# Deferring the dV products of the last head group by two macro steps in an attention backward kernel

## The chip, the cores and the metric

The kernel runs on one core of one Trainium2 chip. The metric is the device time of the program in microseconds; lower is better.

The names are those of the profile: PE is the engine that multiplies matrices, DVE the vector engine, ACT the scalar engine; POOL issues the stores here. A matmul writes into a bank of the memory called PSUM, and an eviction is the copy by DVE or ACT that empties the bank. The granted clock is the share of the full PE clock that the trace records.

## The reference, cut to what matters

The program computes a forward and a backward pass through two rounds of grouped-query attention with a long key/value cache, each followed by an MLP, with shared weights.

```python
def _A_ref(x, k_cache, v_cache, wq, wo):          # B=2, Hq=32, Hkv=4, Sk=16384, Dh=128
    q = (x @ wq).reshape(B, Sq, Hq, Dh)...
    scores = einsum("bhqd,bhkd->bhqk", q, k) * (Dh ** -0.5)
    p = softmax(scores)
    o = einsum("bhqk,bhkd->bhqd", p, v)
    return o... @ wo

x = x + A(layernorm(x)); x = x + B(layernorm(x))  # and both once more
out, vjp = jax.vjp(f, A_x, A_k_cache, A_v_cache, A_wq, A_wo, B_w1, B_b1, B_w2, B_b2)
return (out, *vjp(grad_out))                      # dK and dV: 2 x 4 x 16384 x 128 bf16 each
```

The two cache gradients are 33.5 MB each (2 x 4 x 16384 x 128 x 2 bytes); all outputs together are the 98.6 MB that the profile counts as written.

## The kernel before

The last part of the kernel walks over 32 chunks: 8 pairs of batch and key/value head ("groups"), 4 chunks each, of 4096 key positions. Chunk 31 is the last chunk of the last group. For every chunk it must

- transpose V, form the scores of the gradient (`dp`) and from them `dX`,
- sum dq from `dX` and K (`dq_quad`), and once per group reduce it (`Acc.reduce`),
- form dK and dV of the chunk (`kv_pair`, in two halves) and store 1 MB each.

When both groups of a head are reduced, that head's quarter of dWq can be formed (16 products of 512 columns, `dw_units`) and the gradient that flows on to x (`dn`, 64 matmuls). After the loop comes the backward of the first layer norm and one last small output row.

A half of dK or dV is eight matmuls into four PSUM banks, then four evictions, shared by ACT and DVE. A dWq product is one matmul into one bank and one eviction. All of them take their banks in turn from the same four:

```python
X = [px([128, 512], F32, "xm%d" % i) for i in range(4)]
def mx():
    return nxt("x", X)                            # round robin

def kv_pair(w, i, h):                             # half h of dK or dV of chunk i
    ...
    pss = [mx() for _ in range(4)]
    for b in range(2):
        for r in range(4):
            PE.matmul(pss[r][:, b * 256:(b + 1) * 256], lhsT=blk[32 * r:32 * r + 32, o + 2 * h + b, :],
                      rhs=Qm[...], start=True, stop=True, tile_position=(32 * r, 0))        # L1159
    for r in range(4):
        evac_cast(sv_[:, 2 * h:2 * h + 2, r], pss[r][:]..., 512)                          # L156 ACT, L159 DVE
    if h == 1:
        store(...)                                                                        # L982, 1 MB
# dw_units: one product
    ps = mx()
    PE.matmul(ps[:], lhsT=xrows[p:p + 4, ...], rhs=yrows[p:p + 4, ... 512 columns])          # L1018
    evac_cast(sv_[:, j, c0:c0 + 512], ps[:], 512)
```

The main loop, one macro step per turn. `v_at` says at which step a dV chunk starts, `k_at` the same for dK:

```python
v_at = {2 * i - 3: i for i in range(2, NC)}       # NC = 32 chunks, NCH = 4 per group
k_at = {(i if i < NCH else 2 * i - NCH): i for i in range(NC)}
while 2 * m < NS + 12 or late or fill or late_pe or m <= max(v_at) + 2:
    ...
    for k in range(2):
        ...                                       # transposes of V, scores; dX of a chunk
        if late_pe and (k == 1 or s >= NS):
            late_pe.popleft()()                   # among others the 64 dn matmuls (L847)
        at, w, m_ = ((k_at, "K", m - 1), (v_at, "V", m))[k]
        for h in range(2):
            if at.get(m_ - h) is not None:
                kv_pair(w, at[m_ - h], h)
    ...
    make_blks(iv, ik)                             # transposes the coefficients of the next dV, dK (L1134)
    sch.run_slot(1)                               # the dq work due in this step; the reduce (L426)
    step_fill(1 if m < NCH else 5)                # up to five dW products
    m += 1
g0 = attn_in_bwd(0, g1, dn0)                      # layer norm backward, then the last output row (L195)
```

In the kernel before, the last dq is reduced at the end of step 59; the halves of dV chunks 28 to 31 run in steps 53 to 60.

Of the kernel before, what the change touches and what calls it, by code (L numbers as in the profile page):

```python
# [23 lines left out]
def kernel(  # L24
# [42 lines left out]
    NCH = T // TC  # L67
# [965 lines left out]
    NC = len(chunks)  # L1033
# [248 lines left out]



    v_at = {2 * i - 3: i for i in range(2, NC)}
    k_at = {(i if i < NCH else 2 * i - NCH): i for i in range(NC)}
    NS = (NC - NCH) * NB
    m = 0
    while 2 * m < NS + 12 or late or fill or late_pe or m <= max(v_at) + 2:
# [6 lines left out]
        for k in range(2):  # L1296
            s = 2 * m + k
            if s < NS:
                i, b = NCH + s // NB, s % NB
# [57 lines left out]
```

## Time and profile before

| | kernel before |
|---|---|
| time, median of the first 3 runs | 1173.21 us (1172.8 to 1175.07) |
| read, written | 348 MB, 98.6 MB; DMA 383 GB/s on average |
| last load landed | 1128.6 us |
| last but one reduce of dq, last reduce | 1112.48 us, 1146.22 us |
| issue of the last output row, end | 1168.05 us, 1172.1 us |

First, stretches of the trace of the kernel before. The columns are the stretch, its length, busy time (and count) of PE, PE weight loads, DVE, ACT and POOL, then the granted TensorE clock, the DMA share and GB/s.

```profile
1119.50:1122.70 3.20, 3.19 (x66) 2.24 (x64) 2.33 (x4) 2.09 (x5) 0.53 (x1) 1.00 1.00 412
1122.70:1127.10 4.40, 4.11 (x79) 2.95 (x81) 3.96 (x8) 3.71 (x8) 0.53 (x1) 1.00 1.03 430
...
1112.48:1146.22 33.74, 27.60 (x429) 17.20 (x429) 26.11 (x44) 24.33 (x48) 4.27 (x8) 0.84 1.01 423
...
1146.22:1156.38 10.16, 7.73 (x96) 4.61 (x97) 4.47 (x11) 3.90 (x8) 0.53 (x1) 0.50 0.48 198
1156.38:1161.90 5.52, 5.27 (x12) 1.52 (x11) 4.16 (x8) 4.07 (x8) 1.30 (x2) 0.50 0.92 374
```

Up to the last reduce (1146.22) the DMA is full. Behind it, it is not: between 1146 and 1156 its share is 0.48. The DMA view of the last 32 us, in 40 slices of 0.8 us, shows the hole:

```profile
GB/s 410 430 430 430 420 420 420 461 399 430 379 317 317 225 72 82 51 41 31 20 31 389 430 430 348 399 451 271 379 404 369 323 394 394 287 26 5 0 10 0
```

Seven slices, 5.6 us, are below 150 GB/s. The stores explain it. This is the timeline of POOL, which issues them (start, duration, what; in brackets how long POOL had been idle and what ended that):

```profile
1141.38 0.53 POOL L982 DMA_DIRECT2D out_dram<-keepxK  x1 [4.88 <-DVE keepxK L159]
1143.26 0.53 POOL L982 DMA_DIRECT2D out_dram<-keepK  x1 [1.35 <-ACT blk L148]
1155.81 0.53 POOL L982 DMA_DIRECT2D out_dram<-keepV  x1 [12.02 <-DVE keepV L159]
1157.69 0.53 POOL L982 DMA_DIRECT2D out_dram<-keepK  x1 [1.34 <-ACT big L156]
1159.53 0.77 POOL L982 DMA_DIRECT2D out_dram<-big  x1 [1.31 <-ACT big L156]
1162.58 0.77 POOL L982 DMA_DIRECT2D out_dram<-big  x1 [2.27 <-ACT big L156]
1168.05 0.55 POOL L195 DMA_DIRECT2D out_dram<-o_row  x1 [4.70 <-DVE o_row L194]
```

For 12 us POOL has nothing to store, because the engines are on the chain behind the last dq: reduce, rows of dq, dWq, dn. The chain of waits says the same (start, duration, what):

```profile
1146.22 1.03 PE xm L426 x4
...
1147.86 1.02 PE tpm L949 x8
1148.88 0.02 issue
1148.91 0.59 ACT rowsA L148
1149.49 0.04 issue
1149.54 1.86 PE xm L1018 x4
1151.40 1.82 PE xm L847 x64
1153.22 0.74 PE xm L1159 x7
...
1156.39 3.91 PE xm L1018 x9
```

The twelve last dWq products run back to back; the timeline of PE has them as one line, 12 in 5.27 us:

```profile
1156.39 5.27 PE L1018 MATMUL xm<-rowsA,rowsB 4*128 4x512 bf16 x12 [0.49 <-ACT keepK L156]
```

### The profile page before, as it was taken

To read this page: it belongs to the slowest core of one execution; us is meant where nothing else is said; L and a number is where in the kernel's file an instruction comes from. 1 tells how busy PE (TensorE), PEld (TensorE's weight loads), DVE (VectorE), ACT (ScalarE), POOL (GpSimd) and SP (SyncE) were. 2 spreads that over 40 slices of the span, in tenths; PEclk is the share of its full clock that TensorE was granted. 3 is DMA by queue.
4 is the path that set the end of the run, shared out by engine and by line. 5 is a ranking of instruction groups with operands and counts; after the bars stand their busy time and mean duration, and the time that the engine had idled before them with its cause. 6 is when DMAs were issued, how large, how long until landed. Compare 5 with 4: busy or idle time off the path is not lost. (4 is left out here: it accounts for less than half of the span.)

```text
span 1172.1 us, 40218 instructions
## 1 busy us (share of the span) xinstructions
PE 968.7 (83%) x17709; PEld 743.1 (63%) x17709; DVE 627.2 (54%) x1319; ACT 555.1 (47%) x1395; POOL 63.9 (5%) x113
## 2 busy tenths in 40 slices
PE   4988885497879876899987889888898999898886
PEld 3866673487767755888775688755555554555452
DVE  1544451133545433454845434567777877886774
ACT  0544441022535430344454434367667867786673
POOL 0000000000000000000000000001111111111111
PEclk9988885587989975999997899888777867887785
DMA  9999999998999989989999989677999999999996
GB/s 370 415 417 416 418 417 396 395 356 351 416 417 413 416 329 416 390 320 398 387 410 411 352 320 338 254 271 322 361 403 419 414 417 421 418 421 418 422 423 263
DMA packets 89131, 449.32 MB, mean 383 GB/s; under 512 B 7026, under 2 KB 7026, under 8 KB 49788
## 3 DMA queue, kind: packets, MB, share of 16 engines
q1 hardware_dynamic: 72204, 348.17, 74.5%
q0 software_dynamic: 16752, 98.59, 20.5%
q8 instruction: 138, 2.26, 0.8%
q14 instruction: 37, 0.30, 0.1%
HBM read 348.14 MB, written 98.58 MB: 381 GB/s over the span
## 5 line engine op out<-in xcount | busy, mean ns | idle before, releaser
L148 ACT COPY kT<-tp 128x512 int32<-128x512 int32 x204 | 120.0, 588 | 254.5 <-PE tp L379 246.6
L151 DVE COPY kT<-tp 128x1024 bf16<-128x1024 bf16 x164 | 112.1, 690 | 117.1 <-PE tp L379 106.9
L379 PE MATMUL tp<-ident,kv_K 128*128 128x128 bf16 x1728 | 144.2, 232 | 4.2 <-DMA kv_K<-in_A_k_cache_dram 4.1
L379 PEld LDWEIGHTS <-kv_K 128*128 128x128 bf16 x1728 | 109.6, 104 | 5.0 <-DMA kv_K<-in_A_k_cache_dram 4.7
L159 DVE CAST big<-xm 128x512 bf16<-128x512 f32 x141 | 91.9, 686 | 33.6 <-PE xm L1018 15.9
L156 ACT CAST big<-xm 128x512 bf16<-128x512 f32 x156 | 84.8, 595 | 24.2 <-PE xm L1018 14.7
L532 PEld LDWEIGHTS <-kT 128*128 128x128 bf16 x2048 | 76.6, 98 | 28.3 <-issue 22.3
L532 PE MATMUL sc<-qT_bf,kT 128*128 128x8 bf16 x2048 | 92.1, 171 | 0.7 <-issue 0.7
L263 PE MATMUL wtp<-ident,wt 128*128 128x128 bf16 x928 | 79.3, 235 | 3.8 <-issue 2.4
L379 PE MATMUL tp<-ident,kv_V 128*128 128x128 bf16 x864 | 72.9, 233 | 9.9 <-DMA kv_V<-in_A_v_cache_dram 8.3
L297 PEld LDWEIGHTS <-wt 128*128 128x128 bf16 x1696 | 48.9, 103 | 45.8 <-issue 14.7
L496 ACT ACTIVATE e_all<-sc,negm 128x64 bf16<-128x64 f32 x256 | 77.2, 345 | 1.1 <-DVE negm L491 1.0
L411 PE MATMUL acc_all<-kv_V,e_all 128*16 128x256 bf16 x864 | 46.4, 295 | 28.4 <-DMA kv_V<-in_A_v_cache_dram 15.4
L148 ACT COPY wT<-wtp 128x512 int32<-128x512 int32 (+1 forms) x60 | 34.5, 576 | 74.1 <-PE wtp L263 65.4
L151 DVE COPY wT<-wtp 128x1024 bf16<-128x1024 bf16 (+1 forms) x64 | 40.5, 637 | 52.7 <-PE wtp L263 49.3
L159 DVE CAST keepK<-xm 128x512 bf16<-128x512 f32 x92 | 59.9, 685 | 16.3 <-PE xm L1159 9.4
L156 ACT CAST keepK<-xm 128x512 bf16<-128x512 f32 x105 | 56.2, 593 | 23.3 <-PE xm L1159 21.1
L379 PEld LDWEIGHTS <-kv_V 128*128 128x128 bf16 x864 | 57.5, 104 | 11.8 <-DMA kv_V<-in_A_v_cache_dram 9.2
L263 PEld LDWEIGHTS <-wt 128*128 128x128 bf16 x928 | 60.7, 105 | 4.6 <-issue 3.1
L156 ACT CAST keepV<-xm 128x512 bf16<-128x512 f32 (+1 forms) x98 | 53.3, 595 | 20.3 <-PE xm L1159 17.0
L496 ACT ACTIVATION_READ_ACCUMULATOR e_all<-sc,negm 128x1 f32 x256 | 60.1, 235 | 0.0
L159 DVE CAST keepV<-xm 128x512 bf16<-128x512 f32 (+1 forms) x74 | 48.5, 686 | 20.3 <-PE xm L1159 16.1
(335 smaller groups left out, 1776.2 us busy)
## 6 DMA issues: line engine op xcount, KB each, us to landing
kv_K<-in_A_k_cache_dram SPq DMA_DIRECT2D x81, 1024.0 KB, 12.9
kv_V<-in_A_v_cache_dram SPq DMA_DIRECT2D x81, 1024.0 KB, 12.6
out_dram<-big POOLq DMA_DIRECT2D x36, 1024.0 KB, 17.7
wt<-in_A_wo_dram SPq DMA_DIRECT2D x32, 1024.0 KB, 11.0
wt<-in_B_w_dram SPq DMA_DIRECT2D x32, 896.0 KB, 14.4
out_dram<-keepK POOLq DMA_DIRECT2D x22, 1024.0 KB, 17.6
out_dram<-keepV POOLq DMA_DIRECT2D x18, 1024.0 KB, 17.7
wt<-in_A_wq_dram SPq DMA_DIRECT2D x16, 1024.0 KB, 9.3
```

The source lines that it names most:

```text
L148: S.copy(out=dst.bitcast(I32), in_=src.bitcast(I32))
L151: V.tensor_copy(out=dst, in_=src)
L156: S.copy(out=dst, in_=src)
L159: V.tensor_copy(out=dst, in_=src)
L263: PE.transpose(tp[:, o, :], wv[:, j, (o0 + o) * 128:(o0 + o + 1) * 128], ident[:])
L297: PE.matmul(fps[:, jo, :].rearrange("p (a b) -> p a b", b=2), lhsT=wv[:, j, jo * 128:(jo + 1) * 128], rhs=xT_bf[:, j0 + j, :].unsqueeze(1) ...
L379: PE.transpose(tp[:, j, :], cv[:, b * 8 + j, :], ident[:])
L411: PE.matmul(self.acc[cg:cg + 16, :], lhsT=coef(u), rhs=self.cv[:, t:t + 2, :].rearrange("p t d -> p (t d)"), start=False, stop=True, tile_ ...
L496: S.activation(out=e_all[:, g, f * half:(f + 1) * half, l, h, :], in_=sc[g][f][:, h, :].rearrange("p (a b) -> p a b", b=2), func=ACT.Exp, ...
L532: PE.matmul(sc[g][f][:, :, t % TH], lhsT=kT[:, j, :], rhs=q_bf[:, g, :], start=True, stop=True)
```

## The change

The intent: take the dV products of the last group out of the way of the last dq, so that the chain behind dq starts earlier, and let them run behind it.

```diff
-    v_at = {2 * i - 3: i for i in range(2, NC)}
+    v_at = {2 * i - 3 + (2 if i >= NC - NCH else 0): i for i in range(2, NC)}
```

The eight halves of chunks 28 to 31 move from steps 53 to 60 to steps 55 to 62. The last reduce stays in step 59. Seven of them were issued before it; now five are.

## The prediction

> **What bounds the kernel now.** Over the whole span the DMA engines are full (page, slices: DMA 9 tenths in nearly all). Only the end differs. In the table by stretches, 1000 to 1140 us has a DMA share of 1.01 to 1.03, 1140 to 1150 0.97, 1150 to 1160 0.45, 1160 to 1172 0.65. By the DMA records the last load has landed at about 1128.6 us, and from then to 1149 the stores drain a backlog at 1 MB per 2.47 us. The queue is empty from about 1149 to 1156: the timeline shows dK/dV stores issued at 1141.4 and 1143.3, the next one at 1155.8, then 1157.7, 1159.5 and 1162.6. The tail is a serial chain, not bandwidth: last dq (1146.2) -> dq rows (rowsA 1148.9) -> dWq products, 64 dn matmuls (1151.3 to 1153.2), the last dK and dV halves, the rest of dWq (12 matmuls, 1156.4 to 1161.7, one per 0.43 us), layer norm, output row issued at 1168.05. The last dWq store lands about 1168.2, the row 1169.3.
>
> **What the change does.** No arithmetic is added or removed. Of each of the four dV chunks of the last group, the two halves (8 matmuls, 4 evictions each) run two macro steps later. Net: two dV halves and four coefficient transposes leave the steps at about 1119 to 1127 us, and two halves go behind the last dq, between the dWq products; their coefficients get an eviction of their own.
>
> **Gain.** In 1119.5 to 1127.1 PE is busy 3.19 of 3.20 and 4.11 of 4.40 us, ACT and DVE about 80%. Two halves take 0.40 to 0.69 us of PE each, the four transposes 0.38, the eight evictions 2.1 us of ACT and 2.6 us of DVE in parallel. Estimate: the last dq is reached 2.3 us earlier (1.4 to 3). Loads cannot hold it up: the last K chunk has landed 9 us before its use at 1137.75.
>
> **Cost.** Behind dq the granted clock is 0.5 and the dWq products already hold PE at 5.26 of 5.6 us. A half put between them needs the four PSUM banks that dWq uses, 0.61 us of matmuls and 1.07 (ACT) or 1.29 us (DVE) of evictions. In 1136 to 1146 such a half takes about 1.75 us. Estimate: 1.6 us each, and 0.4 us for the separate coefficient transposes: 3.6 us.
>
> **Sum.** The tail ends about 1.3 us later. The DMA gap gets shorter (stores restart at about 1153.5 instead of 1155.8), but 5 MB instead of 4 MB then remain: at the 2.7 us per MB of the tail it ends near 1169, so bandwidth gives nothing.
>
> The clock: the records switch between 0.5 and 1.0 in multiples of 3.413 us, as the Trainium skill has it ("TensorE: Matmul & The Clock Gate", Part 1). The drop at 1138.8 may fall one window earlier or later against the work; I allow half a microsecond.
>
> **Prediction: 1174.5 us, 1171.5 to 1177.0 in 8 of 10. Faster by over 2%: 0.01; within 2%: 0.98; slower by over 2%: 0.01.**
>
> **Right if:** reduce of the last dq starts at about 1144; the dK store follows at 1153 to 1154; each dV half among the dWq products costs 1.4 to 1.8 us; the last dWq store is issued at 1163.5 to 1164.5; the DMA gap shrinks by 2 to 3 us, with the span no shorter.
>
> **Wrong if:** the removed halves free 3 us or more before dq (then about 0, or a small gain); the dV halves fill waits among the dWq products for nearly nothing (gain of up to 2 us); the clock stays at 1.0 in the tail.

## The result and the profile after

The changed kernel took 1177.39 us (median of 4, 1175.98 to 1178.91), the kernel before 1174.14 us in its 4 runs. The ratio is 1.0027 with a 95% interval of 1.0006 to 1.0049. A second measurement with more rounds gave 1.0045 (1.0022 to 1.0068). Ratios here are the mean time of one kernel's fast runs over that of the other's fast runs of the same rounds, so they are not quite the ratio of the medians quoted. So the change is slower, by some 3 to 5 us, well within 2%.

The same stretches, cut at the same events, of the changed kernel:

```profile
1114.74:1146.43 31.69, 26.61 (x410) 16.09 (x410) 23.45 (x40) 21.74 (x44) 3.72 (x7) 0.86 0.99 411
...
1146.43:1156.71 10.28, 8.10 (x100) 4.83 (x101) 4.74 (x12) 3.96 (x8) 0.53 (x1) 0.50 0.20 80
1156.71:1166.90 10.19, 8.03 (x28) 2.32 (x27) 7.37 (x13) 6.20 (x12) 1.83 (x3) 0.50 0.78 309
```

Its timeline of PE over the last dWq products:

```profile
1156.71 2.29 PE L1018 MATMUL xm<-rowsA,rowsB 4*128 4x512 bf16 x5
1158.39 1.22 PE L1159 MATMUL xm<-QmV,blkv 32*128 32x256 bf16 x3
1159.78 0.58 PE L1159 MATMUL xm<-QmV,blkv 32*128 32x256 bf16 x5 [0.17 <-DVE big L159]
1160.91 2.35 PE L1018 MATMUL xm<-rowsA,rowsB 4*128 4x512 bf16 x5 [0.55 <-ACT keepxV L156]
1162.65 1.22 PE L1159 MATMUL xm<-QmV,blkv 32*128 32x256 bf16 x3
1164.04 0.58 PE L1159 MATMUL xm<-QmV,blkv 32*128 32x256 bf16 x5 [0.17 <-DVE big L159]
1165.16 1.01 PE L1018 MATMUL xm<-rowsA,rowsB 4*128 4x512 bf16 x2 [0.55 <-ACT keepxV L156]
```

And its stores, and the DMA view from 1140 us to the end (40 slices of 0.93 us):

```profile
1156.02 0.53 POOL L982 DMA_DIRECT2D out_dram<-keepV  x1 [12.23 <-DVE keepV L159]
1157.80 0.53 POOL L982 DMA_DIRECT2D out_dram<-keepK  x1 [1.25 <-ACT blkv L148]
1159.49 0.76 POOL L982 DMA_DIRECT2D out_dram<-keepK  x1 [1.15 <-ACT keepK L156]
1166.34 0.53 POOL L982 DMA_DIRECT2D out_dram<-keepxV  x1 [6.09 <-DVE keepxV L159]
1167.45 0.76 POOL L982 DMA_DIRECT2D out_dram<-big  x1 [0.58 <-issue]
1172.98 0.53 POOL L195 DMA_DIRECT2D out_dram<-o_row  x1 [4.77 <-DVE o_row L194]
```

```profile
GB/s 381 292 328 416 425 407 416 416 142 106 44 27 27 44 18 27 27 0 275 416 407 319 425 407 328 376 390 58 0 151 416 425 323 390 381 182 5 0 9 0
```

What the reader is to see:

- From the last but one reduce to the last: 31.69 us instead of 33.74. The steps ahead of the last dq did get shorter.
- From the last reduce to the next dWq products, 10.28 instead of 10.16 us: nothing gained, nothing lost.
- Then the twelve products. In the kernel before they take 5.5 us with their evictions. Here two halves stand between them, and it takes 10.2 us. The start of the sixth product of the stretch is 2.54 us behind the fifth (11.94 and 14.48 us behind the reduce, in the trace's instruction records) where it is 0.43 us in the kernel before. So one half costs 2.11 us.
- The store of the last dWq part goes out 21.0 us behind the reduce (1167.45 less 1146.43) instead of 16.4.
- The hole in the DMA did not shrink. It grew: ten slices of 0.93 us below 150 GB/s, 9.3 us, and a second hole near 1166 us. Counted in the same way in three traces of each program (table below), the first hole is 5.6, 6.4 and 6.4 us before and 9.3, 7.4 and 9.3 us with the change.

Three traces of each program give the sizes. (The third trace with the changed order is the experiment without the last dV store, below, whose engines do the same.)

| us | before | change |
|---|---|---|
| start of the last but one reduce (nothing differs up to there) | 1112.48, 1117.85, 1114.42 | 1114.74, 1116.43, 1118.89 |
| from it to the last reduce | 33.74, 33.94, 33.94 | 31.69, 32.66, 32.73 |
| from the last reduce to the issue of the output row | 21.83, 21.85, 21.84 | 26.55, 26.56, 26.56 |
| sum of the two | mean 55.71 | mean 58.92 |
| from the issue of the row to the end | 4.10 in all three | 4.07, 4.07, 4.01 |

The first row is scatter that the change has no part in, 1112 to 1119 us. The third row repeats to 0.02 us. The difference of the sums, +3.2 us, is the effect by the traces: 1.5 us less ahead of the last dq, 4.7 us more behind it.

The 1.5 us need not all be due to the order. In the three traces of the kernel before, the granted clock is 0.5 for one stretch of 3.41 us just behind the last but one reduce, and in the third trace of the change too (32.73 us). In the first two traces of the change there is no such stretch (31.69 us, and 32.66 us with a wait for a load that is shown below). Compared under the same clock the gain is 33.87 less 32.73, 1.1 us; that is one trace of the change. The part behind the last reduce runs at 0.5 throughout in all six.

### The profile page after: what moved, and what is told of

Same layout as the page of the kernel before. It is cut to its first block, busy times and chain, and to the rows that moved or that the text cites. A ratio compares the mean times of both kernels' runs of the same rounds, so it can differ in the third digit from the quotient of the medians.

```text
span 1177.1 us, 40223 instructions
## 1 busy us (share of the span) xinstructions
PE 970.7 (82%) x17709; PEld 740.9 (63%) x17709; DVE 628.3 (53%) x1320; ACT 553.7 (47%) x1395; POOL 63.7 (5%) x113
## 5 line engine op out<-in xcount | busy, mean ns | idle before, releaser
L159 DVE CAST big<-xm 128x512 bf16<-128x512 f32 x137 | 89.3, 685 | 26.7 <-PE xm L1159 13.0
L156 ACT CAST big<-xm 128x512 bf16<-128x512 f32 x152 | 82.2, 593 | 23.0 <-PE xm L1018 11.1
L379 PE MATMUL tp<-ident,kv_V 128*128 128x128 bf16 x864 | 70.4, 228 | 8.0 <-DMA kv_V<-in_A_v_cache_dram 6.4
L263 PEld LDWEIGHTS <-wt 128*128 128x128 bf16 x928 | 59.7, 104 | 5.4 <-issue 4.0
```

Source lines behind the costliest of these rows:

```text
L156: S.copy(out=dst, in_=src)
L159: V.tensor_copy(out=dst, in_=src)
L263: PE.transpose(tp[:, o, :], wv[:, j, (o0 + o) * 128:(o0 + o + 1) * 128], ident[:])
L379: PE.transpose(tp[:, j, :], cv[:, b * 8 + j, :], ident[:])
```

## The experiments

Theory P (place): a dV half is cheap where it was and dear where it went, because among the dWq products it has to share four PSUM banks with them and each waits for the other's evictions. Rival W (write bandwidth): more stores are left when the queue restarts, and writing them ends the program. Rival D (drift): the profiled run of the change was 2.3 us late at the last but one reduce already, so there may be no effect at all.

### The change again

> The changed kernel again, to size the effect with more rounds. Theory P (place: two dV halves cost about 2.05 us each among the dWq products plus 0.6 us for their own coefficient transposes, 4.7 us in all, and give back only about 2.05 us before the last dq): +2.6 us, ratio 1.0022, and in the profile 31.7 us from the reduce of the last dq but one to that of the last (33.7 in the kernel before), then 26.5 us to the issue of the output row (21.8 before). Rival W (write bandwidth: 5 MB instead of 4 MB left when the stores restart): about the same total, but the last row would have to wait for stores, not for engines. Rival D (drift: the profiled run of the change was already 2.3 us late at the last dq but one, where nothing has changed yet): ratio within 1.000 to 1.001.

Measured: 1180.88 us (median of 6), the kernel before 1174.06 us, ratio 1.0045 (1.0022 to 1.0068). In the trace 32.66 us between the reduces and 26.56 us from the last one to the row. The tail is as expected to 0.1 us; the gain ahead of it is smaller. One line of the waits of PE in this stretch names an item that the first trace did not have:

```profile
PE tpm L1304 <- DMA keepK<-in_A_v_cache_dram: 1.2, 1, 1.2
```

PE had got ahead of a load of V and waited 1.2 us for it. D falls: the ratio is outside its 1.000 to 1.001.

### Only the last chunk later

```diff
-    v_at = {2 * i - 3: i for i in range(2, NC)}
+    v_at = {2 * i - 3 + (2 if i == NC - 1 else 0): i for i in range(2, NC)}
```

> The kernel before with the last dV chunk alone two macro steps later. P: nothing is taken out of the busy steps at 1119 to 1127 us; one half leaves the step of the last dq (worth about 1.7 us), one the step after it (about 1.7), two go among the dWq products (4.1 us) with 0.6 us of transposes: +1.3 us (0.7 to 2). W: 4 MB remain at the restart as in the kernel before, so 0 to +0.3 us.

Measured: ratio 0.999 (0.9964 to 1.0015), which decides nothing. The trace does more: 31.79 us between the reduces, 24.78 us to the row, 56.57 in sum, +0.9 us against the kernel before, inside P's range and above W's. The two halves stand in the dWq products exactly as in the change:

```profile
1159.13 2.29 PE L1018 MATMUL xm<-rowsA,rowsB 4*128 4x512 bf16 x5
1160.81 1.22 PE L1159 MATMUL xm<-QmV,blkv 32*128 32x256 bf16 x3
1162.20 0.58 PE L1159 MATMUL xm<-QmV,blkv 32*128 32x256 bf16 x5 [0.17 <-DVE big L159]
1163.32 2.35 PE L1018 MATMUL xm<-rowsA,rowsB 4*128 4x512 bf16 x5 [0.55 <-ACT keepxV L156]
```

Again 2.54 us from product to product (10.16 and 12.70 us behind the reduce). One half has left the step behind the reduce, so the first product of the stretch starts 8.50 us behind it instead of 10.16 in the kernel before. That is 1.66 us less; against the change, which also has the separate coefficient transposes there, it is 1.78 us less (10.28). So a half costs about 1.7 to 1.8 us there, with the next half waiting for it, and 2.1 us is more than that.

### Six PSUM banks in the tail, changed kernel

```diff
         sch.s = m
         qs = []
+        if m == 2 * NC - 5:
+            X.extend(t[:].bitcast(F32).rearrange("p a b -> p (a b)") for t in TP)
         iv, ik = v_at.get(m + 1), k_at.get(m)
```

`TP` are the two banks that the transposes use; hardly any are left in the tail.

> The changed kernel with six PSUM banks instead of four in rotation from the step of the last dq on. P with the PSUM round trip as its mechanism: a dV half among the dWq products no longer waits for their evictions and they not for its own; it costs 1.0 to 1.3 us instead of 2.05, so 1.5 to 2 us less than the change, about +0.5 to +1 us against the kernel before. If a half cost what its matmuls and evictions take, whatever the banks: no change, +2.6 us. W: no change, +2.6 us.

Measured: 1175.76 us against 1180.88 for the change on the same chip in the same rounds; ratio to the kernel before 1.0002 (0.9979 to 1.0024). From the last reduce to the row 23.74 us instead of 26.56. The timeline of PE over the first half among the dWq products:

```profile
1154.69 0.63 PE L1018 MATMUL xm<-rowsA,rowsB 4*128 4x512 bf16 x1
1154.71 0.90 PE L1159 MATMUL xm<-QmV,blkv 32*128 32x256 bf16 x2
1155.25 0.39 PE L1159 MATMUL tpm<-QmV,blkv 32*128 32x256 bf16 x2
1155.26 0.56 PE L1159 MATMUL xm<-QmV,blkv 32*128 32x256 bf16 x2
1155.62 1.06 PE L1018 MATMUL xm<-rowsA,rowsB 4*128 4x512 bf16 x2
```

From 1154.69 to 1155.62 it is 0.93 us from product to product, instead of 2.54; the half costs 0.5 us. The waits for the evictions in brackets, of 0.17 and 0.55 us, are gone. The work is the same: same matmuls, same evictions, same clock of 0.5. So 1.6 of the 2.1 us were waits for a PSUM bank, not work. The expectation for the half (1.0 to 1.3 us) was still too dear.

### Six banks, kernel before

The same edit in the kernel before.

> The control: six banks in the kernel before. The three halves and the dWq products behind the last dq go a little faster: 0.5 to 1 us less than the kernel before. P with round trips: the distance between the two placements falls from 2.6 to at most 1.7 us. W: 0, and the distance stays at 2.6.

Measured: ratio 0.9984 (0.9957 to 1.0011); 20.46 us from the last reduce to the row instead of 21.84. (Behind the last dq there are two halves ahead of the twelve products, not three.) The expected 2.6 and 1.7 us were differences of the whole. From the last but one reduce to the row the difference of the two placements is 54.56 - 53.23 = 1.3 us with six banks and 3.2 with four, as expected; but only the trace of `before_six` has the stretch of half clock ahead of the last dq, so part of this is not the banks. From the last reduce to the row alone it is 23.74 - 20.46 = 3.3 us with six banks and 4.7 with four. Of these 3.3 us the two halves are 1.0, the last product to the row 0.8 (7.83 against 7.02), and the rest is the first dWq product behind the coefficient transposes: it starts 10.19 us behind the reduce against 8.75 in the kernel before, 1.4 us more, where the difference was 0.1 us with four banks. The transposes now share their bank with the rotation, and in `after_six` this product waits for their eviction:

```profile
1153.03 0.58 PE L1018 MATMUL tpm<-rowsA,rowsB 4*128 4x512 bf16 x1 [0.69 <-ACT blkv L148]
```

What the six banks save in the tail is not all saved in the total. The row of `before_six` is issued at 1164.10 us and the program ends 6.18 us later instead of 4.10 (5.48 in `after_six`):

```profile
1164.10 0.55 POOL L195 DMA_DIRECT2D out_dram<-o_row  x1 [4.71 <-DVE o_row L194]
```

In its packet records the row's packets are done by 1165.7 us, and a single chain of 4 KB packets runs on alone to 1167.5. So with a tail only 1.4 us shorter the stores already end the program in this trace: from the last but one reduce to the end it takes 59.41 us, against 59.66 to 59.89 in the kernel before.

### Six banks after the coefficient transposes

The edit above with `m == 2 * NC - 3`, two steps later.

> The changed kernel with the two further PSUM banks in rotation only one macro step before the end, after the coefficient transposes that use one of them. If the costs add as read: a dV half among the dWq products delays them by 0.5 us instead of 2.1, and the transposes stay at 0.1 us, so 23.3 us (22.9 to 23.8) from the last reduce to the issue of the output row, against 26.56 in the change and 21.83 in the kernel before.

Measured: 24.68 us, 0.9 us above the top of the expected range. The transposes stay at 0.1 us as expected, and the second half costs 0.56 us. But the first half costs 1.36: when it comes, the four old banks have just been taken by dWq products and only the two new ones are free, so it waits for evictions again. The miss agrees with the mechanism: which banks are free when the half comes counts, not the number of banks alone.

### No store of the last dV chunk

The changed kernel without one store of 1 MB. Its result is wrong: the last chunk of dV stays unwritten.

```diff
             dst = dVv if w == "V" else dKv
+            if (w, i) == ("V", NC - 1):
+                return by_store.append(stgs[w, i])
             store(dst[g, :, c * TC:(c + 1) * TC, :], ...)
```

> The changed kernel without the store of the last dV chunk (1 MB; the result is wrong on purpose, the chunk stays unwritten). W: 2.5 us less than the change, back to the kernel before. P: the engines' chain is untouched, within 0.5 us of the change, so +2 to +2.6 us against the kernel before.

Measured: ratio 1.0042 (1.0014 to 1.0069), no faster than the change; 26.56 us from the last reduce (1151.62) to the row, then 4.0 us to the end. Its last stores:

```profile
1172.64 0.76 POOL L982 DMA_DIRECT2D out_dram<-big  x1 [7.20 <-issue]
1178.18 0.55 POOL L195 DMA_DIRECT2D out_dram<-o_row  x1 [4.77 <-DVE o_row L194]
```

The last dWq store goes out 21.02 us behind the reduce, as in the change, although one megabyte less is written. W falls as an explanation of the change.

### The dq work first in each of the last steps

```diff
+            if m > NS // 2 and k == 0:
+                sch.run_slot(1)
             at, w, m_ = ((k_at, "K", m - 1), (v_at, "V", m))[k]
 ...
-        sch.run_slot(1)
+        if m <= NS // 2:
+            sch.run_slot(1)
         step_fill(1 if m < NCH else 5)
```

> The kernel before, with the dq work of each of the last steps issued ahead of that step's dK and dV halves instead of behind them. P (the tail is a serial chain with idle gaps of 3.3 us between the last dq and the first dWq eviction): two halves fill that gap, 2 to 3 us less than the kernel before. W (the tail is bound by writing): at most 1 us less.

Measured: ratio 0.9987 (0.9962 to 1.0011). In the trace 30.04 + 23.87 = 53.91 us, 1.8 us less than the kernel before's 55.71. The direction is P's; the size is a little under its range.

### The last dq one step earlier

`dq_first`, and both quads of the last chunk in the same step:

```diff
-        sch.later(2, lambda: dq_quad(i, 1))
+        n = 1 if i == NC - 1 else 2
+        sch.later(n, lambda: dq_quad(i, 1))
         if c == NCH - 1:
-            sch.later(2, accs[g].evac)
-            sch.later(3, accs[g].reduce)
+            sch.later(n, accs[g].evac)
+            sch.later(n + 1, accs[g].reduce)
```

> As dq_first, and the last dq sums both its quads one macro step earlier, so that dWq runs among the last dK and dV halves. P: 3 to 5 us less than the kernel before; the idle gap of the stores shrinks, by the DMA records, from 6.6 to under 4 us. W: at most 1 us less.

Measured: 1173.60 us, ratio 0.9975 (0.9947 to 1.0002). From the last but one reduce to the end 57.8 us, against 59.7 to 59.9 in the three traces of the kernel before: 2.0 us less, not 3 to 5. The hole in the stores is still 5.7 us in this trace (slices below 150 GB/s). A dK half and a dV half now stand between the fifth and the sixth of the twelve products, which start 4.33 us apart: about 1.95 us for each half, with waits for evictions as in the change.

> dq_early once more, for a narrower interval: 2 us less than the kernel before (ratio 0.998), as its trace has it from the reduce of the last dq but one to the end (57.8 against 59.6 us); the first runs gave 0.9975 with an interval that just reaches 1.

Measured: 1173.30 us against 1175.92 us, ratio 0.9973 (0.9952 to 0.9995); from the last but one reduce to the end 58.4 us, 1.4 us less than the kernel before. The hole in the stores is 2.5 us in this trace, so the shrinking that was expected is seen in one of two. This kernel is correct, and of all that were run it is the one with a measured gain over the kernel before, of about a quarter of a percent. On the second measurement the interval leaves out 1; on the first it just does not.

### Both: the last dq earlier and six banks

> As dq_early with six PSUM banks in rotation in the tail. P with round trips: another 1 to 2 us less than dq_early. Without them: no difference to dq_early.

Measured: ratio 1.0004 (0.9974 to 1.0034), with runs from 1171.6 to 1181.1 us, so no gain is shown over `dq_early`. The engines did get faster: the row is issued 22.90 us behind the last reduce instead of 27.69, and from the last but one reduce to the row it is 48.25 us against 53.71. But from the row to the end it is 9.2 us instead of 4.1. The DMA view of its last 30 us, in slices of 0.75 us:

```profile
GB/s 448 306 339 426 448 371 393 426 382 382 262 240 142 76 33 126 377 388 366 393 459 371 459 388 366 426 366 388 388 366 49 22 22 27 27 27 5 0 0 11
```

Here, as in the two six-bank kernels above, the stores end the program, not the engines. From 1167.5 to about 1172 us some 25 GB/s are still moving: in the packet records that is one chain of 4 and 8 KB packets, each starting where the last one ends. So W is wrong for the change, but stores do end the program where six banks made the tail short: from the row to the end it takes 5.48 us in `after_six`, 6.18 in `before_six` and 9.2 here. At the very end it is not the full write bandwidth that is used up, but this one chain that lags; why it does was not tested.

## Why the prediction was right or wrong

The prediction said 1174.5 us with a range up to 1177.0. The median was 1177.39, so it was outside. It started from 1173.21 us for the kernel before, which came out at 1174.14 with a fourth run; 0.9 us of the miss are that. The direction and the mechanism of the tail held, the sizes did not, and the forecast for the DMA gap was wrong.

- "The tail is a serial chain, not bandwidth": right. Without one of the stores the tail took the same 26.56 us.
- "Estimate: the last dq is reached 2.3 us earlier (1.4 to 3)": too high. Measured 1.5 us on average (33.87 less 32.36; single traces 1.0 to 2.3), and 1.1 us in the one trace under the same clock. In one of the traces 1.2 us of it went into a wait for a load. "Loads cannot hold it up" looked only at the last K chunk; it was a V chunk that PE waited for.
- "Estimate: 1.6 us each": this is the step that failed most. A half among the dWq products costs 2.11 us, 4.2 us for both. The estimate took what a half costs next to other halves (1.7 to 1.8 us by the run with only the last chunk moved). Between single-bank products it is worse: the half must wait until the products in front of it have left the four banks, and the next product waits for the half's first eviction.
- "0.4 us for the separate coefficient transposes": too high. They run while PE waits for a bank anyway; 0.12 us.
- Not foreseen: from the last dWq product to the row it takes 7.44 us instead of 7.02. The layer norm starts on DVE. In the kernel before, the last product is evicted by ACT, and the layer norm starts 0.84 us behind the start of that product. With the change, DVE gets this eviction, and the layer norm starts behind it, at 1.27 us. Together 0.12 + 4.18 + 0.42 = 4.72 us, which is the measured difference; the prediction had 3.6.
- "The tail ends about 1.3 us later": 3.2 us by the traces, made of 0.8 us less gain and 1.1 us more cost.
- "The DMA gap gets shorter": wrong. It grew from 5.6 to 6.4 us to 7.4 to 9.3. The dV store that was deferred is missing from the backlog in front of the gap (between the two reduces, the timeline of POOL has eight stores before and seven with the change), so the queue runs dry earlier, while the next store comes no earlier behind the last reduce (9.59 us in both kernels). The run with only the last chunk moved still has eight stores there, and supports this: by the packet records, no more than three packets are in flight from 39.2 us behind the last but one reduce on, from 38.6 to 38.9 us in the kernel before, but from 34.4 to 37.2 us with the change.
- The range also ignored the scatter. It was built on three runs within 2.3 us; the kernel before later ran from 1170.2 to 1181.6 us. The change's second measurement, some 5 us slower than the kernel before by its ratio, is consistent with the 3.2 us of the traces (its interval begins at 2.6 us), but what the rest of it is, if it is anything, stays open.

## What to carry to other kernels

Moving work off a critical chain pays only for what it frees where it was, and costs what it takes where it goes. Price it in both places, with the buffers it will share there: here the same half of dV cost 2.1 us behind single-bank products in a rotation of four PSUM banks, and 0.5 us with six, or 1.4 us with six when the free banks came in the wrong order. Then look at what comes next: when the tail got shorter, the stores ended the program. When the effect is a few tenths of a percent, measure between two events of one trace: the total scattered by 11 us, the tail by 0.02 us.

## What the Trainium skill lacked or had wrong

- "Perfetto Trace Analysis", Matmul Optimizations, advises to use all 8 PSUM banks for parallelism. Both kernels already do (their PSUM pools hold 2, 4, 1 and 1 buffers). What the page lacks is how to divide them, and what that is worth: two more banks in the rotation cut the cost of a four-bank half between single-bank products from 2.11 to 0.51 us. There is a catch: a bank shared with the transposes made the next transposes cost 1.4 us instead of 0.1.
- "TensorE: Matmul & The Clock Gate", Part 1, says that the clock is halved after an idle window of about 3.4 us and comes back after one busy window. The steps of 3.413 us between 0.5 and 1.0 are as the page has them. But in the kernel before, the clock fell at 1138.8 us behind a window (1135.36 to 1138.77) with matmuls for 1.67 of 3.41 us and no wait over 0.8 us, and it stayed at 0.5 through the stretch from 1156.38 to 1161.90 with PE busy for 5.27 of 5.52 us. The products themselves agree with the record: one starts every 0.43 us there, and every 0.21 us in `dq_early` where the record shows 1.0. The page gives no measure of how little work makes a window idle. Those products use 4 of 128 rows; whether that is why was not tested.
- "Perfetto Trace Analysis", What "DMA-bound" means, names specific DMA engines as one bound. The end of the last experiment fits it (one chain of packets at about 25 GB/s for 4 us behind the rest; 2 us in `before_six`). That the chain belongs to one DMA engine is not shown, the page gives no size for such a lag, and no run here tested its cause.
